# Weight preparation of a second FFN tied to program order, its output weights split at use, and token pairs in another order

## The chip, the cores and the metric

The kernel runs on one core of one Trainium2 chip. The metric is the device time of one execution in microseconds (us); lower is better.

## The reference, cut to what matters

```python
a = attention(q, mean_pool8(k), mean_pool8(v))      # 8 batches, 8 heads, 576 tokens, width 64
x = a as (4608 tokens, 512)
h = x @ w_in;  x = max(0.01 * h, h) @ w_out         # first FFN, 512 -> 2048 -> 512
xn = x / sqrt(mean(x * x) + 1e-6) * rms_g
g, val = xn @ w_gate, xn @ w_val                    # second FFN, 512 -> 1536
out = (g * sigmoid(g) * val) @ w_out2               # 1536 -> 512
```

The activations are fp32. The weights arrive as 64-bit floats, and the kernel turns them into fp32 itself.

## The kernel before, in words

Every product is made of three matmuls of rounded parts: a number is kept as a high part (an fp32r copy) and a low part (the rest), and `TERMS` names high x high, high x low and low x high. `split` (L89) makes the two parts: a copy on ACT for the high one, a subtraction on POOL or DVE for the low one.

**First stage.** Nine tiles of 512 tokens (loop at L1090). In each, 16 jobs `f`: `h_unit` (12 matmuls, then two activations on ACT and a subtraction on DVE) and, two jobs later, `y_unit` (12 matmuls). Attention for the coming tiles runs beside this: its steps are written into `attention_slot` (L1110), which is called twice in a job, so there are 32 slots to a tile. `y_store` ends a tile. Half of the first FFN's output weights (`wr`, L674) are loaded again in every tile from tile 2 on, so that eight of these weights take turns in four slots, and four slots are free.

**Preparation of the second FFN's weights**, `side_steps` (L682). From tile 2 on, each slot also runs one entry of a list of steps. A unit of work takes a raw tile of 64-bit words (512 KB): `start` loads it (SP), `convert` starts to make fp32 of it (an activation on ACT, L98, and a multiplication on DVE, L692), `end` merges the halves (DVE, L698) and, for gate and value weights, makes four sums (L709), `high` and `low` split into parts (ACT L735, POOL L739), and `store` writes them to DRAM (SP, L745: `op_dram` for gate and value, `wo_dram` for the output weights, here in the trace `op_g`, `op_v` and `wo`). There are 24 units for gate and value, each six slots behind the last, and 12 for the output weights, each four slots behind the last. Two slots hold raw tiles (`raws`) in turn and two (`outs`) hold parts.

**Second stage.** Five pairs of token blocks (L794): three of 2 x 512 tokens, then two of 2 x 384. For each pair there are 12 `Quad`s (6 of gate, 6 of value in turn); a quad makes seven products of six matmuls where eight would be usual (`p1` to `p7`), with the sums prepared above. Its weights come from DRAM in four loads to a quad, into ten slots `a` (`load_a`, L934). The products of a value quad become the inputs `u` of the output product, in which each of 12 `f` takes 12 matmuls (9 in a pair of 384) for each half of the pair. These are cut into `pieces` (`queue_out`, L1154), one or two of which run in a quad; the rest, the second half of the pair above all, runs after the quads, and four pieces are left for the next pair. The output weights `wo` of each `f` are loaded for each half (`load_o`, L953): 120 loads into four slots `o`, three `f` ahead. Norm and token sums of the next pair run between the products (`norm_steps`, `token_steps`).

**Order.** The program is traced in this order, and a scheduler then orders each engine's instructions by a simulated timeline; an instruction whose inputs are ready early by that timeline can be moved ahead. Each engine, and the queue of DMA issues on SP, then works in the order given, and one that waits holds up what is behind it. `keep_in_program_order(ins)` puts `ins` behind the instruction that was traced just before it on its engine, without a wait for its end.

**What the change touches:** `prelu` (L97), the copies `er` in attention's `step_x` (L362), `wo_dram` (L664), `side_steps`, `pairs`, `load_a`, `load_o`, `first_pair` (L962), `queue_out` and the loop over quads (L1162).

Of the kernel before, what the change touches and what calls it, by code (L numbers as in the profile page):

```python
# [22 lines left out]
def pooled_attention_then_two_ffns(  # L23
# [73 lines left out]
    def prelu(out, in_, alpha, scale=1.0):  # L97
        nc.scalar.activation(out=out, in_=in_, func=AF.Prelu, scale=scale, alpha=alpha)  # L98
# [248 lines left out]
    def step_x(b, t):  # L347
# [14 lines left out]
        for g in range(2):  # L362
            (nc.scalar.copy if b < 2 else nc.gpsimd.tensor_copy)(  # L363
# [300 lines left out]
    wo_dram = [dram.tile([P, 2, 512], F32, name=f"wo{f}") for f in range(F2)]  # L664
# [17 lines left out]
    def side_steps():  # L682
# [13 lines left out]
        def merge(raw):  # L696
            top, low = raw[:, :, 1], raw[:, :, 0]
            nc.vector.scalar_tensor_tensor(  # L698
                out=top, in0=top, scalar=3, in1=low, op0=ALU.logical_shift_left, op1=ALU.bitwise_or
            )  # L700
# [13 lines left out]
        def unit(begin, n, name, load, srcs_of, with_sums):  # L714
# [3 lines left out]
            def start():  # L718
                held["raw"] = raw_in_slot(raws[n % 2], f"raw_{name}")
                load(held["raw"])  # L720

            def end():
                merge(held["raw"])
                if with_sums:
                    sums(held["raw"].bitcast(F32).rearrange("p (k i n) w -> p k i n w", k=2, i=2))

            def high(z):
                t = weight_slot(outs[z], f"parts_{name}_{z}").rearrange("p h n -> p (h n)")
                held[z], o = [], 0
                for src, dst in srcs_of(held["raw"])[z]:  # L730
                    a, b = src.shape[1:]
                    d = t[:, o:o + 2 * a * b].rearrange("p (a h n) -> p a h n", a=a, h=2)
                    o += 2 * a * b
                    held[z].append((src, d, dst))
                    nc.scalar.activation(out=d[:, :, HI, :], in_=src, func=AF.Copy)  # L735

            def low(z):
                for src, d, dst in held[z]:
                    nc.gpsimd.tensor_tensor(  # L739
                        out=d[:, :, LO, :], in0=src, in1=d[:, :, HI, :].bitcast(F32), op=ALU.subtract  # L740
                    )

            def store(z):
                for src, d, dst in held[z]:
# [3 lines left out]
            at(begin + 3, lambda: convert(held["raw"]))  # L748
            at(begin + 4, end)
            for z, t0, t2 in ((0, 5, 8), (1, 7, 10)) if with_sums else ((1, 6, 9),):  # L750
                at(begin + t0, lambda z=z: high(z))
                at(begin + t0 + 1, lambda z=z: low(z))
                at(begin + t2, lambda z=z: store(z))

        begin = n = 0
        for p in range(NPAIR):
            for m, src in (("g", w_gate), ("v", w_val)):
                for c in range(2):
                    def load(raw, src=src, p=p, c=c):
                        nc.sync.dma_start(  # L760
                            out=raw.rearrange("p (k f) w -> p k (f w)", k=2),
# [467 lines left out]
```

## Time and profile before

| | us |
|---|---|
| median of 3 runs | 1883.0 |
| lowest, highest | 1882.14, 1887.19 |
| profiled execution | 1877.53 |
| its span, first to last instruction | 1875.8 |

PE is the matmul engine (TensorE), PEld its weight loads, DVE VectorE, ACT ScalarE, POOL GpSimd, SP the engine that issues DMAs; a q behind the name is an engine's sequencer. A line of code stands as L592, a tile by its name without numbers, and `out<-in` says what an instruction writes and reads. The granted clock is that of TensorE, 1.00 being 2.4 GHz. A wait is put down to what ended last before the waiting instruction began.

### The profile page before, as it was taken

What the parts mean: (1) busy time and instruction counts of PE and PEld (TensorE: products, weight loads), DVE (VectorE), ACT (ScalarE), POOL (GpSimd) and SP (SyncE); (2) the same over time, 40 slices, a digit from 0 to 9 for tenths busy, and PEclk for the clock granted to TensorE, in tenths of its full rate; (3) what the DMA queues carried; (4) which work ended last, traced back from release to release, by engine and by line L of the source; (5) the groups of instructions that cost most, each with busy time, mean ns of one, the idle gap of its engine ahead of it and who ended that gap; (6) DMA issues with size and microseconds to landing.
All of it is one profiled execution on the core that took longest, in us unless ns stands there. A gap on an engine that the chain in (4) does not pass through costs nothing.

```text
span 1875.8 us, 23874 instructions
## 1 busy us (share of the span) xinstructions
PE 1777.5 (95%) x8596; PEld 1500.1 (80%) x8596; DVE 858.4 (46%) x1533; ACT 671.3 (36%) x1424; POOL 575.7 (31%) x751
## 2 busy tenths in 40 slices
PE   4899989989999999999999999999999999999898
PEld 3789877767888888888887787878787888898886
DVE  8975457567344344343162456145513451443232
ACT  5754355454333333332343323232313232332221
POOL 2654246446213131000122432243213322330340
PEclk9999998989999999999999999999999999999999
DMA  8833268778533332212243556765676567777754
GB/s 263 291 103 97 76 205 275 239 244 264 192 99 85 97 92 82 68 46 79 90 130 123 181 180 204 248 197 185 197 244 201 182 216 256 236 241 254 236 201 157
DMA packets 173733, 330.82 MB, mean 176 GB/s; under 512 B 54320, under 2 KB 88112, under 8 KB 172848
## 3 DMA queue, kind: packets, MB, share of 16 engines
q1 hardware_dynamic: 173616, 329.31, 54.1%
q8 instruction: 68, 1.11, 0.2%
q14 instruction: 49, 0.40, 0.1%
HBM read 277.87 MB, written 51.38 MB: 176 GB/s over the span
## 4 chain that ended last, share of the span: by engine, by line
PE 71%; DMA 11%; DVE 9%; POOL 3%; issue 2%; ACT 2%; SPq 1%; POOLq 0%; ACTq 0%; DVEq 0%
PE h L592 15%; PE y L628 15%; PE o L1077 14%; PE yv L1002 5%; PE yg L1002 4%; PE xv L1002 3%; PE xg L1002 3%; PE wg L1002 3%; PE wv L1002 3%; DMA av<-op_v 2%; DMA raw_v<-in_moe_w_val_dram 2%; DMA ag<-op_g 1%; PE sc L325 1%; PE av L395 1%; DMA wo<-parts_p 1%
## 5 line engine op out<-in xcount | busy, mean ns | idle before, releaser
L592 PE MATMUL h<-xhl,w_i 128*128 128x512 f32 (+1 forms) x1824 | 438.1, 385 | 1.4 <-ACT w_i L92 0.7
L592 PEld LDWEIGHTS h<-xhl,w_i 128*128 128x128 f32 x1824 | 330.4, 191 | 65.6 <-DVE xhl L95 2.5
L1077 PE MATMUL o<-wo,u 128*128 128x512 f32 x1296 | 320.8, 392 | 10.7 <-DMA wo<-wo 4.6
L1077 PEld LDWEIGHTS o<-wo,u 128*128 128x128 f32 x1296 | 241.0, 188 | 64.9 <-DMA wo<-wo 6.1
L628 PE MATMUL y<-ghl,w_o 128*128 128x512 f32 (+1 forms) x1296 | 286.0, 366 | 1.4 <-DVE ghl L605 1.4
L628 PEld LDWEIGHTS y<-ghl,w_o 128*128 128x128 f32 x1296 | 220.0, 192 | 35.5 <-DVE ghl L605 1.8
L605 DVE TENSOR_TENSOR ghl<-g,ghl 128x512 fp32r<-128x512 f32 (+1 forms) x152 | 111.8, 736 | 203.9 <-ACT g L98 200.2
L628 PE MATMUL y<-ghl,wr 128*128 128x512 f32 x624 | 158.3, 395 | 0.0
L98 ACT ACTIVATE ghl<-h 128x512 fp32r<-128x512 f32 (+1 forms) x152 | 86.7, 570 | 167.9 <-PE h L592 164.6
L628 PEld LDWEIGHTS y<-ghl,wr 128*128 128x128 f32 x624 | 115.2, 188 | 22.5
L95 POOL TENSOR_TENSOR u<-e2g,u 128x512 fp32r<-128x512 f32 (+1 forms) x25 | 31.1, 1244 | 213.6 <-ACT u L92 213.6
L1002 PE MATMUL xv<-xa,av 128*128 128x512 f32 (+1 forms) x360 | 85.6, 371 | 7.5 <-DMA av<-op_v 7.5
L1018 POOL TENSOR_TENSOR e7g<-e7v,e7g 128x512 f32<-128x512 f32 (+1 forms) x25 | 29.5, 1179 | 204.3 <-DVE e7v L979 204.3
L1002 PE MATMUL xg<-xa,ag 128*128 128x512 f32 (+1 forms) x360 | 85.4, 370 | 7.0 <-DMA ag<-op_g 3.8
L363 POOL COPY er<-ex 128x96 f32<-128x96 f32 x60 | 18.7, 339 | 227.0 <-DVE ex L340 227.0
L92 ACT ACTIVATE u<-e7g 128x512 fp32r<-128x512 f32 (+1 forms) x30 | 17.7, 590 | 193.2 <-POOL e7g L1018 177.1
L98 ACT ACTIVATE g<-h 128x512 f32<-128x512 f32 (+1 forms) x152 | 86.7, 570 | 0.0
L229 POOL TENSOR_TENSOR v<-v 128x256 f32<-128x256 f32 (+2 forms) x84 | 56.8, 679 | 93.7 <-DMA v<-in_v_dram 91.5
L1002 PE MATMUL yg<-T,ag 128*128 128x512 f32 (+1 forms) x360 | 84.3, 368 | 0.0
L1002 PE MATMUL yv<-T,av 128*128 128x512 f32 (+1 forms) x360 | 84.1, 368 | 0.1
L1002 PEld LDWEIGHTS xv<-xa,av 128*128 128x128 f32 x360 | 65.7, 188 | 19.5 <-DMA av<-op_v 10.2
L1002 PEld LDWEIGHTS xg<-xa,ag 128*128 128x128 f32 x360 | 65.5, 188 | 19.0 <-ACT e2g L1011 3.5
(166 smaller groups left out, 2706.7 us busy)
## 6 DMA issues: line engine op xcount, KB each, us to landing
wo<-wo SPq DMA_DIRECT2D x120, 512.0 KB
av<-op_v SPq DMA_DIRECT2D x90, 512.0 KB
ag<-op_g SPq DMA_DIRECT2D x90, 512.0 KB
wr<-wo SPq DMA_DIRECT2D x52, 512.0 KB
y<-ye SPq DMA_DIRECT2D x36, 256.0 KB
op_g<-parts_g SPq DMA_DIRECT2D x36, 256.0 KB
op_v<-parts_v SPq DMA_DIRECT2D x36, 256.0 KB
out_dram<-oe SPq DMA_DIRECT2D x36, 256.0 KB
```

The lines of the kernel that those rows point to most:

```text
L95: lo_eng.tensor_tensor(out=lo, in0=src, in1=hi.bitcast(F32), op=ALU.subtract)
L98: nc.scalar.activation(out=out, in_=in_, func=AF.Prelu, scale=scale, alpha=alpha)
L229: nc.gpsimd.tensor_tensor(out=x[:, :n], in0=x[:, :n], in1=x[:, n:2 * n], op=ALU.add)
L325: nc.tensor.matmul(pt[:, i * n:(i + 1) * n], y[:, p, :], kblk[b % 2][:, p * n:(p + 1) * n], start=True, stop=True,)
L363: (nc.scalar.copy if b < 2 else nc.gpsimd.tensor_copy)(out=er[:, g].rearrange("p d (q k) -> p d q k", q=2), in_=e[:, 2 * g:2 * g + 2, P:]. ...
L395: nc.tensor.matmul(pt[:, :n], vb[b, p][:, sp].rearrange("p h d -> p (h d)"), a[:, p, mp, 0:n], start=i == 0, stop=False,)
L592: nc.tensor.matmul(pt, w[:, sp, c * P:(c + 1) * P], x[:, mp, c, :], start=c == 0 and i == 0, stop=c == n_k - 1 and i == 2,)
L605: nc.vector.tensor_tensor(out=t[:, LO, :], in0=g, in1=t[:, HI, :].bitcast(F32), op=ALU.subtract)
L628: nc.tensor.matmul(pt, w[:, sp, m * P:(m + 1) * P], g[:, mp, a - c0:a - c0 + n], start=ydone[j, a] == 1 and i == 0 and m % per_bank == 0, ...
L1002: nc.tensor.matmul(pt, wt[:, a, c, sp, :], xt[:, mp, :], start=start and c == 0 and i == 0, stop=c == 1 and i == 2, skip_group_check=not s ...
L1018: eng.tensor_tensor(out=s, in0=src, in1=s, op=ALU.mult)
L1077: nc.tensor.matmul(pt, u[:, sp, m * P:(m + 1) * P], w[:, mp, :], start=f == 0 and i == 0, stop=f == F2 - 1 and i == 2,)
```

## The change

It does five things.

1. The load of a raw tile and the activation of `convert` are put in program order. `convert` comes five slots behind the load, in the same slot as `end`; before, it came three behind, and `end` four. The parts follow from the sixth slot on.
2. The output weights of the second FFN are no longer split when they are prepared: a unit ends with the merge into a slot of `outs`, and 256 KB are stored in place of 512.
3. They are split when used: `load_o` loads 256 KB into the low half of a slot, and `split_o` makes both parts there (copy on ACT, subtraction on POOL), one `f` ahead of the matmuls. The 12 loads for the second half of the last pair go to the slots `a` behind all of `load_a`'s own; in the last two quads of the last pair one piece fewer runs each.
4. The pairs are of 512, 384, 512, 384 and 512.
5. The copies `er` of batches 2 to 7 run on DVE and not on POOL.

```diff
     def prelu(out, in_, alpha, scale=1.0):
-        nc.scalar.activation(out=out, in_=in_, func=AF.Prelu, scale=scale, alpha=alpha)
+        return nc.scalar.activation(out=out, in_=in_, func=AF.Prelu, scale=scale, alpha=alpha)
...
-            (nc.scalar.copy if b < 2 else nc.gpsimd.tensor_copy)(
+            (nc.scalar.copy if b < 2 else nc.vector.tensor_copy)(
...
-    wo_dram = [dram.tile([P, 2, 512], F32, name=f"wo{f}") for f in range(F2)]
+    wo_dram = [dram.tile([P, 512], F32, name=f"wo{f}") for f in range(F2)]
...
-            prelu(top.bitcast(F32), top.bitcast(F32), 2.0 ** 32, scale=2.0 ** -112)
+            tc.keep_in_program_order(
+                prelu(top.bitcast(F32), top.bitcast(F32), 2.0 ** 32, scale=2.0 ** -112)
+            )
...
+        def load_raw(n, name, out, src):
+            t = raw_in_slot(raws[n % 2], f"raw_{name}")
+            tc.keep_in_program_order(nc.sync.dma_start(out=out(t), in_=src))
+            return t
...
             at(begin, start)
-            at(begin + 3, lambda: convert(held["raw"]))
-            at(begin + 4, end)
-            for z, t0, t2 in ((0, 5, 8), (1, 7, 10)) if with_sums else ((1, 6, 9),):
+            at(begin + 5, lambda: convert(held["raw"]))
+            at(begin + 5, end)
+            for z, t0 in ((0, 6), (1, 8)):
                 at(begin + t0, lambda z=z: high(z))
                 at(begin + t0 + 1, lambda z=z: low(z))
-                at(begin + t2, lambda z=z: store(z))
+                at(begin + t0 + 3, lambda z=z: store(z))
+
+        def plain(begin, n, f):
+            held = {}
+
+            def start():
+                held["raw"] = load_raw(
+                    n, f"p{f}", lambda t: t.rearrange("p n w -> p (n w)"), rows(w_out2, f)
+                )
+
+            def end():
+                held["t"] = per.tile([P, 2, 512], F32, tag=f"w{outs[n % 2]}", bufs=1, name=f"plain{f}")[:, 0, :]
+                merge(held["raw"], held["t"].bitcast(I32))
+
+            at(begin, start)
+            at(begin + 5, lambda: convert(held["raw"]))
+            at(begin + 5, end)
+            at(begin + 6, lambda: nc.sync.dma_start(out=wo_dram[f], in_=held["t"]))
...
-    pairs = [(0, N), (2 * N, N), (4 * N, N), (6 * N, N - P), (8 * N - 2 * P, N - P)]
+    pairs = [(0, N)]
+    for n in (N - P, N, N - P, N):
+        pairs.append((pairs[-1][0] + 2 * pairs[-1][1], n))
...
+    a_todo += o_todo[-F2:]
+    del o_todo[-F2:]
...
+            a_count[0] += 1
+            if len(a_todo[i]) == 3:
+                load_o_into(a_todo[i], "a", i)
+                return
...
+    def load_o_into(key, kind, i):
+        t = slot(kind, i, f"wo{key[0]}_{key[1]}_{key[2]}")
+        nc.sync.dma_start(out=t[:, LO, :].bitcast(F32), in_=wo_dram[key[2]])
+        o_tiles[key] = t
+        o_whole.append((key, t))
...
+    def split_o(key):
+        for x in [x for x in o_whole if x[0] <= key]:
+            o_whole.remove(x)
+            t = x[1]
+            split(nc.scalar, t[:, HI, :], nc.gpsimd, t[:, LO, :], t[:, LO, :].bitcast(F32))
...
                 if ms[0] == 0:
                     load_o()
+                    if (q, z) == (last_q, 1):
+                        load_a()
+                    split_o(o_order[min(i + 1, len(o_order) - 1)])
                 out_part(q, z, f, ms)
...
-            if i + 1 < len(quads):
+            if i + 1 < (len(quads) if more else len(quads) - 2):
                 piece()
```

## Rows read from the trace of the kernel before

**Rows 1.** The page: busy share by engine, and TensorE's clock in 40 slices.

```profile
PE 1777.5 (95%) x8596; PEld 1500.1 (80%) x8596; DVE 858.4 (46%) x1533; ACT 671.3 (36%) x1424; POOL 575.7 (31%) x751
...
PEclk9999998989999999999999999999999999999999
```

**Rows 2.** Windows, tiles 1-5, 7: PE, PEld, DVE, ACT, POOL busy (count), clock, DMA share, GB/s.

```profile
173.70:288.50 114.80, 106.31 (x513) 87.95 (x512) 60.21 (x129) 49.83 (x118) 45.06 (x80) 0.97 0.49 145
288.50:411.80 123.30, 110.02 (x513) 89.86 (x513) 77.78 (x163) 61.84 (x149) 67.12 (x103) 0.94 0.79 252
411.80:512.90 101.10, 96.55 (x445) 79.93 (x445) 55.55 (x100) 42.98 (x99) 47.62 (x72) 0.99 0.72 234
512.90:615.10 102.20, 102.20 (x504) 85.62 (x503) 41.13 (x81) 35.28 (x79) 23.61 (x54) 1.00 0.32 97
615.10:719.20 104.10, 103.63 (x512) 86.68 (x510) 41.34 (x85) 36.09 (x84) 24.68 (x54) 1.00 0.31 93
...
823.60:920.40 96.80, 96.80 (x461) 81.10 (x460) 29.02 (x60) 27.40 (x56) 2.10 (x6) 1.00 0.20 68
```

**Rows 3.** Waits of PE in tiles 1 to 3: total us, times, longest us.

```profile
PE qt L303 <- issue: 10.2, 4, 4.0
PE xt L369 <- DVE ex L340: 8.7, 2, 5.3
PE av L395 <- DVE at L95: 5.3, 3, 2.6
```

**Rows 4.** Waits of PE in tiles 4 to 8 (512.9 to 1008 us), all of them.

```profile
PE av L395 <- DVE at L95: 1.2, 2, 0.7
```

**Rows 5.** Waits of DVE and of SP's queue, 213 to 493 us.

```profile
DVE raw_v L692 <- DMA raw_v<-in_moe_w_val_dram: 20.2, 8, 5.8
...
SPq L745 <- POOL parts_v L739: 45.3, 38, 3.8
```

**Rows 6.** Tile views of raw_g, parts_p: duration ns min/median/max, first and last start.

```profile
L760 SPq DMA_DIRECT2D raw_g<-in_moe_w_gate_dram x12: 367/381/386, 213.0 to 456.1; - x12
...
L735 ACT ACTIVATE parts_p<-raw_p x12: 657/670/694, 258.8 to 491.0; 128x512 fp32r<-128x512 f32 x12
L739 POOL TENSOR_TENSOR parts_p<-raw_p,parts_p x12: 1304/1316/1843, 259.5 to 491.8; 128x512 fp32r<-128x512 f32 x12
```

**Rows 7.** Waits of PE in the last two pairs, 1541.7 us to the end.

```profile
PE xv L1002 <- DMA av<-op_v: 7.0, 6, 1.8
PE o L1077 <- DMA wo<-wo: 4.6, 4, 1.3
PE xg L1002 <- DMA ag<-op_g: 3.0, 4, 2.5
```

**Rows 8.** Windows, columns as in rows 2: pairs 1 and 3, an output stretch, the tail.

```profile
1170.50:1359.80 189.30, 185.31 (x808) 150.56 (x807) 79.87 (x113) 58.31 (x97) 60.90 (x47) 1.00 0.63 209
...
1541.70:1698.70 157.00, 151.35 (x769) 136.48 (x768) 61.19 (x107) 47.80 (x94) 47.75 (x47) 1.00 0.72 241
...
1371.00:1391.00 20.00, 20.00 (x90) 16.58 (x89) 1.38 (x2) 0.63 (x1) 0.00 (x0) 1.00 0.64 217
...
1832.00:1875.80 43.80, 35.66 (x158) 28.38 (x156) 9.92 (x18) 3.80 (x7) 0.00 (x0) 0.99 0.48 159
```

**Rows 9.** DMA of the second stage (1008 us to the end): total, and the output weights' loads.

```profile
DMA packets 59274, 183.85 MB, mean 212 GB/s; under 512 B 6336, under 2 KB 9408, under 8 KB 58816
...
wo<-wo SPq DMA_DIRECT2D x120, 512.0 KB
```

**Rows 10.** The chain that ended last: start us, us, what.

```profile
1372.06 17.68 PE o L1077 x78
...
1827.57 2.08 PE o L1077 x9
...
1849.49 5.84 DMA wo<-wo
```

**Rows 11.** Tile view of `er`, columns as in rows 6.

```profile
L363 POOL COPY er<-ex x60: 258/267/727, 191.4 to 873.1; 128x96 f32<-128x96 f32 x60
```

More of the change, by code (lines that the diff above doesn't have):

```diff
@@ L694, in convert, with merge @@
             )
-        def merge(raw):
+        def merge(raw, out):
             top, low = raw[:, :, 1], raw[:, :, 0]
             nc.vector.scalar_tensor_tensor(
-                out=top, in0=top, scalar=3, in1=low, op0=ALU.logical_shift_left, op1=ALU.bitwise_or
+                out=out, in0=top, scalar=3, in1=low, op0=ALU.logical_shift_left, op1=ALU.bitwise_or
             )
@@ L729, in high @@
                 held[z], o = [], 0
-                for src, dst in srcs_of(held["raw"])[z]:
-                    a, b = src.shape[1:]
+                for x, dst in srcs_of(held["raw"])[z]:
+                    a, b = x.shape[1:]
                     d = t[:, o:o + 2 * a * b].rearrange("p (a h n) -> p a h n", a=a, h=2)
                     o += 2 * a * b
-                    held[z].append((src, d, dst))
-                    nc.scalar.activation(out=d[:, :, HI, :], in_=src, func=AF.Copy)
+                    held[z].append((x, d, dst))
+                    nc.scalar.activation(out=d[:, :, HI, :], in_=x, func=AF.Copy)
@@ L758, in side_steps @@
                 for c in range(2):
-                    def load(raw, src=src, p=p, c=c):
-                        nc.sync.dma_start(
-                            out=raw.rearrange("p (k f) w -> p k (f w)", k=2),
-                            in_=src[:, p * 2 * W:(p + 1) * 2 * W].rearrange("(k c p) f -> c p k f", k=2, p=P)[c],
-                        )
                     def srcs(raw, m=m, p=p, c=c):
@@ L771, in srcs @@
                         )
-                    unit(begin, n, f"{m}{p}_{c}", load, srcs, True)
+                    operands(
+                        begin, n, f"{m}{p}_{c}", lambda t: t.rearrange("p (k f) w -> p k (f w)", k=2),
+                        src[:, p * 2 * W:(p + 1) * 2 * W].rearrange("(k c p) f -> c p k f", k=2, p=P)[c], srcs,
+                    )
                     begin += 6
@@ L776, in side_steps @@
             for f in (2 * p, 2 * p + 1):
-                def load(raw, f=f):
-                    nc.sync.dma_start(out=raw.rearrange("p n w -> p (n w)"), in_=rows(w_out2, f))
-                def srcs(raw, f=f):
-                    x = raw.bitcast(F32)[:, :, 1].unsqueeze(1)
-                    return None, ((x, wo_dram[f].rearrange("p h n -> p (h n)").unsqueeze(1)),)
-                unit(begin, n, f"p{f}", load, srcs, False)
+                plain(begin, n, f)
                 begin += 4
@@ L927, in token_steps @@
         ]
+    last_q = len(pairs) - 1
     a_todo = [(q, p, m, s) for q in range(len(pairs)) for p in range(NPAIR) for m in "gv" for s in range(4)]
+    o_todo = [(q, z, f) for q in range(len(pairs)) for z in range(2) for f in range(F2)]
+    a_todo += o_todo[-F2:]
+    del o_todo[-F2:]
     a_tiles = {}
     a_count = [0]
+    o_tiles = {}
+    o_count = [0]
+    o_whole = []
     def load_a():
@@ L975, in first_pair @@
             when.setdefault(13 + i // 2, []).append(load_o)
+        when.setdefault(15, []).append(lambda: split_o((0, 0, 0)))
         return when, late
@@ L1152, in piece @@
             pieces.pop(0)()
+    o_order = [(q, z, f) for q in range(len(pairs)) for z in range(2) for f in range(F2)]
     def queue_out(q, z, f):
```

27 lines of the change are left out of this document (9 added, 18 removed).

## The prediction

> **What bounds the kernel now.** I read the page first. TensorE is busy for 95% of the span and its granted clock is full in all slices but a few [rows 1]. So what can be won is what TensorE loses, and other engines matter only where they make it wait. The row of clocks shows where to look: the dents lie in the first half, around slices 6 to 10.
>
> Next the windows, one to a tile of the first FFN, from the first matmul of a tile's `h` to that of the next. Tiles 1 to 3 are long; tiles 4, 5 and 7 are calm (tile 6 is like tile 5), with TensorE busy throughout at clock 1.00 [rows 2]. Tiles of a like number of TensorE instructions can be compared: tile 5 has 512 in 104.1 us. Tile 1 has 513 and takes 114.8, 10.7 more; tile 2 has 513 and takes 123.3, 19.2 more. Tile 3 has 445. Between tiles 5 and 7 an instruction is worth (104.1 - 96.8) / (512 - 461) = 0.14 us, so 445 would take 94.5, and 101.1 is 6.6 more. **Tiles 1 to 3 lose 36.5 us.**
>
> The waits of TensorE in these tiles say how. Attention's transposes and products waited 10.2 + 8.7 + 5.3 = 24.2 us [rows 3], against 1.2 us in tiles 4 to 8 [rows 4]. The rest is clock: 0.97, 0.94 and 0.99 of the three tiles are 3.4 + 7.4 + 1.0 = 11.9 us. The two make 36.1, so the loss is accounted for twice over: stalls, and the lower clock in the stretches around them.
>
> What runs there and not in the calm tiles is the preparation of the second FFN's weights. Its first load is issued at 213 us and the last `gate` load at 456 [rows 6], though program order puts the first at the start of tile 2 (288.5 us) and the last early in tile 8. The scheduler has moved it up and packed it. DMA share in tile 2 is 0.79 against 0.31 in tile 5 [rows 2]. On DVE's in-order queue the first operation on a raw tile stood waiting for its load, 20.2 us in 8 waits for `raw_v` alone, and SP stood behind stores whose POOL half was not done, 45.3 us for `parts_v` alone [rows 5]. Attention's softmax, and its loads of q, are queued behind these.
>
> In the second stage the windows by pair show two kinds. A pair of 512 columns moves 209 GB/s, one of 384 columns 241 GB/s [rows 8], since weights are loaded whole for less work. In the last two pairs, both of 384, TensorE waits on loads for 7.0 + 4.6 + 3.0 = 14.6 us [rows 7]. The last 43.8 us hold only 35.66 us of TensorE work [rows 8], and the chain that ended last goes through two loads of `wo` there, one of 5.84 us [rows 10].
>
> **Part 1: the preparation is pinned.** The loads (SP) and the `convert` activation (ACT) are ordered behind what was traced before them. The rest of each unit hangs on these by data. 36 units of 6 or 4 slots are 192 slots, 32 to a tile: six tiles and two slots of the seventh, some 630 us in place of 280. Each unit keeps its instructions, except that the 12 of `w_out` lose their split (ACT 670 ns, POOL 1.316 us [rows 6]) and half of their store. `convert` is now five slots, 16 us of a 104 us tile, behind its load, and so no longer arrives before it. What was late next was attention; the calm tiles show that attention alone fits under TensorE. What stays of the 36.5 us is bounded by 0 and by the density: 280 / 630 = 0.44 of it, 16 us. I take 5, since the DMA engines are a third busy in these tiles and there is room between arrivals. **Gain 31.5 us, between 20 and 36.5.** The pinned load also holds nothing back on SP that is due sooner: behind it in program order stand loads of later slots. If the ACT queue comes to a pinned `convert` whose load is late, the `h` activations behind it wait, and TensorE has two units of `h` (12 matmuls each, 2.7 us) before it would feel it.
>
> **Part 2: `er` copies from POOL to DVE.** 60 copies of 267 ns [rows 11]. On DVE the trace has none; between 0 (it fills a wait) and 60 x 0.27 = 16 us of DVE time in tiles where DVE is busy for 41 of 104 us [rows 2]. Taken at nothing for TensorE. It spares a hop, and POOL is free for the pinned units' work.
>
> **Part 3: `wo` halves, split when used.** 120 loads [rows 9] go from 512 to 256 KB, 31 of the second stage's 184 MB. Each now needs an ACT copy and a POOL subtraction: by the same shapes' rows 0.67 and 1.32 us [rows 6], so 80 us of ACT and 158 us of POOL over 865 us. In the second pair POOL is busy for 61 of 189 us and ACT for 58 [rows 8]; 24 splits add 32 and 16 there. They fit by amount. They have to fit by latency where only `o` products are left. There one `f` of a 512 pair is 12 matmuls, 17.68 / 78 x 12 = 2.72 us, and one of a 384 pair is 9, 2.08 us [rows 10]; POOL and ACT are all but idle in such a stretch, 0.00 and 0.63 of 20 us [rows 8]. With four slots a load may be issued three `f` ahead: 8.2 or 6.2 us for the load and 2.0 us of split. Cost: nothing where the load lands within 4.2 us, up to one split (2.0 us) at each of the four pair boundaries where POOL has other work, so 0 to 8; I take 2.
>
> Gain: at the old pace a 384 pair would move 24 x 0.262 = 6.3 MB less in 157 us, 201 GB/s; run without waits (about 140 us) 225, between the pair with hardly a wait (209) and the one with waits (241). I keep 3 of the 14.6 us. **Gain 11.6 us less 2, between -8 and 15.**
>
> A rule speaks against this. The Trainium skill, "DMA: Bandwidth & Descriptors", section "Anatomy of one DMA", gives a transfer a fixed cost of about 2.0 us and only the rest by bytes. By it, as an estimate, a `wo` load would fall only from 3.2 to 2.6 us; if latency and not rate made the waits, this part would give a fifth of the 14.6, 3 us, in place of 11.6.
>
> **Part 4: pairs 512, 384, 512, 384, 512.** The same number of columns and of matmuls, so nothing in TensorE time; two more loads of `xst`, hidden by the quads around them. It puts a light pair behind each heavy one and a light one last, which is part of the 11.6. **Part 5: the last pass's `wo` in the `a` slots, two pieces kept back.** Ten of twelve loads then come before the tail. The tail loses 43.8 - 35.66 = 8.1 us, some 3 of them the last copy and store; the 4.6 us of `wo` waits is already in the sum, nothing is added.
>
> **Sum.** 31.5 + 11.6 - 2 = 41 us. The profiled execution took 1877.5 us, 1.7 more than its span; less 41 this is 1836.5. The median of the runs, 1883.0, lies 5.5 above the profiled one, so 1842.
>
> **The rivals.** *The pin doesn't hold* (0.12): it ties an instruction only to the one just before it on its engine, and if that one (a load of q, say) is itself moved up, the preparation stays packed. For it: SP's loads have few ties. Against: the instruction before a pinned `convert` is often the `h` activation, which can't run before its matmuls. Then part 1 gives some 5 us and the rest 10: 1868.
>
> *Part 3 gives nothing* (0.08): the waits for loads are latency. For it: single `wo` loads of 5.84 us on the chain [rows 10] while the tail moved little. Against: the waits sit in the pairs with the highest rate. Then 1883 - 31.5 = 1851. The skill's fixed cost, above, would make it so.
>
> *Slower* (0.08): load and split together become the bound of the `o` stretches. The place is the 12 `f` of the second half of each pair but the last, whose loads come early. Load 5.84, split 2.0, and one POOL operation of 1.3 ahead of it make 9.1 us; this is 2.9 over the 6.2 us of a 384 pair and 0.9 over the 8.2 of a 512 pair: 24 x 2.9 + 24 x 0.9 = 91 us, so 1883 - 31.5 + 91 = 1942. It outweighs part 1 from a chain of some 7.5 us on (24 x 1.3 = 31). Against: the load is halved and the engines are idle there.
>
> **The numbers.** The forecast has 0.72. A measurement of this kernel can tell some 0.3%, 5.6 us, from no change. The forecast and the first two rivals are all faster, together 0.92; 0.04 of it goes to no change, where the pin fails and the split costs what it saves: 0.88. The low end takes both gains whole: 1883 - 36.5 - 15 = 1831, and 1829 for the small waits beside them. The high end takes 20 us for part 1 and a loss of 2 for part 3: 1865. It leaves out the failing pin and the slower case, together 0.2.
>
> **What would show it.** Loads of raw tiles from the start of tile 2 to tile 8; tiles 1 to 3 at 104, 104 and 95 us (a little more for tile 3), clock 1.00, no waits of `qt` and `xt`. In the second stage waits on `av`, `ag` and `wo` of 3 us in all, and a new wait of `o` on POOL (the split) of 2. Wrong if raw loads still begin before 270 us, if tiles 4 to 7 grow by over 2 us each, or if `o` waits on POOL for over 8 us.

## The result and the profile after

The changed kernel is slower: 1912.4 us (median of 4 runs, 1909.2 to 1916.2) against 1884.5 for the kernel before, ratio 1.0149, 95% interval 1.0124 to 1.0173. The forecast was 1842, in a range of 1829 to 1865.

The page after, head and busy shares; they answer to [rows 1]. ACT has 61 us more work and POOL 124, and TensorE's share is a point lower.

```profile
span 1914.5 us, 24149 instructions
...
PE 1795.0 (94%) x8596; PEld 1506.2 (79%) x8596; DVE 883.7 (46%) x1593; ACT 732.2 (38%) x1532; POOL 699.6 (37%) x799
```

The windows by tile of the kernel after (columns as in [rows 2]), tiles 1 to 7:

```profile
173.10:278.90 105.80, 103.84 (x514) 86.71 (x512) 44.50 (x92) 34.82 (x81) 22.05 (x41) 1.00 0.20 54
278.90:384.10 105.20, 103.40 (x513) 86.79 (x512) 55.48 (x124) 43.28 (x105) 33.47 (x60) 1.00 0.48 154
384.10:482.60 98.50, 95.80 (x446) 79.00 (x445) 41.41 (x88) 34.66 (x79) 31.75 (x52) 1.00 0.47 150
482.60:595.50 112.90, 105.30 (x504) 87.59 (x503) 58.85 (x118) 43.12 (x99) 34.38 (x60) 0.97 0.49 153
595.50:706.50 111.00, 106.28 (x512) 88.40 (x511) 57.86 (x124) 44.87 (x107) 33.44 (x60) 0.97 0.49 151
706.50:816.60 110.10, 107.52 (x513) 89.47 (x511) 56.53 (x125) 44.50 (x106) 18.25 (x32) 0.96 0.42 131
816.60:913.40 96.80, 96.80 (x460) 81.11 (x460) 41.74 (x94) 36.45 (x78) 11.19 (x16) 1.00 0.47 158
```

Tiles 1, 2 and 3 are shorter by 9.0, 18.1 and 2.6 us than in [rows 2]: the pin holds, and the preparation is no longer packed into them but runs on to tile 8. But tiles 4 and 5 are longer by 10.7 and 6.9, and tile 6 by 5.7 (104.4 us before), at a clock of 0.97 and 0.96 where it was 1.00. The second stage begins at 1001.3 us in place of 1008.3: 7 us are left of 36.

The second stage as one window, from the first matmul of its first quad to the last copy of its output, for the kernel before and after:

```profile
1008.30:1872.70 864.40, 831.77 (x3833) 701.92 (x3831) 334.88 (x518) 247.95 (x438) 260.62 (x223) 1.00 0.64 212
```

```profile
1001.30:1911.50 910.20, 851.06 (x3833) 708.62 (x3831) 345.45 (x518) 314.74 (x555) 413.51 (x339) 0.99 0.53 168
```

It is 46 us longer, with fewer bytes (168 GB/s in place of 212), with 67 us more of ACT and 153 more of POOL, against 80 and 158 that were worked out. TensorE's own busy time is 19 us longer for the same 3833 instructions, at a clock of 0.99 in place of 1.00; the rest are waits. **So the first stage gained little and the second lost much.** Two views tell where.

First, the waits of PE in tiles 4 to 6 after, and of DVE between 278 and 905 us:

```profile
PE xt L369 <- DVE ex L340: 7.6, 2, 5.8
PE xr L374 <- DVE er L363: 6.1, 3, 2.1
```

```profile
DVE raw_v L695 <- DMA raw_v<-in_moe_w_val_dram: 42.2, 10, 5.9
DVE raw_p L695 <- DMA raw_p<-in_moe_w_out_dram: 36.8, 12, 6.5
DVE raw_g L695 <- DMA raw_g<-in_moe_w_gate_dram: 36.4, 12, 5.2
```

DVE stands waiting for raw loads 34 times, 115 us in all. Only the ACT half of `convert` is pinned; its DVE multiplication was put right behind the load, where by the scheduler's timeline the load has landed. The timeline of such a place, which holds the longest wait of `xt`:

```profile
514.52 0.46 SPq L719 DMA_DIRECT2D raw_v<-in_moe_w_val_dram  x1
...
519.05 0.43 DVE L695 TENSOR_SCALAR raw_v<-raw_v 128x512 int32<-128x512 uint32 x1 [4.99 <-DMA raw_v<-in_moe_w_val_dram]
519.39 0.20 DVE L339 RECIPROCAL st<-st 128x8 f32<-128x8 f32 x1
519.62 0.76 DVE L340 TENSOR_TENSOR ex<-ex,st 128x576 f32<-128x576 f32 x1
520.41 0.41 DVE L363 COPY er<-ex 128x96 f32<-128x96 f32 x2
520.53 0.87 PE L369 MATMUL xt<-ident,ex 128*128 128x128 f32 x3 [5.75 <-DVE ex L340]
```

The softmax (L339, L340) and the copies `er`, now on DVE too, are queued behind a multiplication whose result is not used before 555.2 us, when the merge begins, 36 us later, and TensorE waits 5.75 us for them. (Just before, L338 had held DVE for 2.91 us where 0.17 is usual; see the last section.)

Second, the second stage: the waits of PE, and the longest of ACT (the kernel before has no wait of ACT for `wo`).

```profile
PE xv L1035 <- DMA av<-op_v: 11.7, 8, 3.1
PE xg L1035 <- ACT e1g L1063: 7.5, 7, 1.3
PE xg L1035 <- ACT e2g L1044: 7.1, 2, 3.7
PE yv L1035 <- DVE e7v L1012: 5.6, 5, 1.8
PE xg L1035 <- ACT rms L873: 5.3, 2, 2.7
```

```profile
ACT wo L92 <- DMA wo<-wo: 181.2, 68, 8.4
```

`av` is waited for no less than before (7.5 us) though the rate has fallen, and new waits stand behind ACT: in all, TensorE waits 57.6 us in this stage in place of 31.1, behind ACT 26.8 in place of 4.3 and behind loads 15.3 in place of 15.9. The timeline of one, in the first pair of 384:

```profile
1224.00 0.63 ACT L92 ACTIVATE wo<-wo 128x512 fp32r<-128x512 f32 x1 [3.96 <-DMA wo<-wo]
1224.64 1.28 ACT L873 ACT_TABLE_LOAD   x1
...
1225.94 0.69 ACT L873 ACTIVATE rms<-ms,eps 128x512 f32<-128x512 f32 x1
...
1226.68 2.29 PE L1035 MATMUL xg<-xa,ag 128*128 128x384 f32 x6 [2.58 <-ACT rms L873]
```

The copy of the split stands 3.96 us in ACT's queue until its load lands; `rms`, which has to empty the bank that the next `xg` writes, is behind it, and a table load of 1.28 us, which the kernel before has too, comes between them.

### The profile page after: what moved, and what is told of

Its sections match the earlier page's. It is cut to its first block, busy times and chain, and to the rows that moved or that the text cites. A ratio compares the mean times of both kernels' runs of the same rounds, so it can differ in the third digit from the quotient of the medians.

```text
span 1914.5 us, 24149 instructions
## 1 busy us (share of the span) xinstructions
PE 1795.0 (94%) x8596; PEld 1506.2 (79%) x8596; DVE 883.7 (46%) x1593; ACT 732.2 (38%) x1532; POOL 699.6 (37%) x799
## 4 chain that ended last, share of the span: by engine, by line
PE 67%; DMA 14%; DVE 9%; POOL 5%; ACT 2%; issue 2%; SPq 1%; POOLq 0%; ACTq 0%; DVEq 0%
PE h L592 16%; PE y L628 15%; PE o L1110 12%; PE yv L1035 4%; PE yg L1035 4%; PE xv L1035 3%; PE xg L1035 3%; PE wg L1035 3%; PE wv L1035 3%; DMA wo<-wo 2%; DMA av<-op_v 2%; DMA v<-in_v_dram 2%; PE sc L325 1%; DMA ag<-op_g 1%; DMA raw_v<-in_moe_w_val_dram 1%
## 5 line engine op out<-in xcount | busy, mean ns | idle before, releaser
L1110 PE MATMUL o<-wo,u 128*128 128x512 f32 x1296 | 325.7, 395 | 12.9 <-POOL u L95 2.9
L95 POOL TENSOR_TENSOR wo<-wo 128x512 fp32r<-128x512 f32 x120 | 159.8, 1334 | 316.2 <-ACT wo L92 315.6
L92 ACT ACTIVATE wo<-wo 128x512 fp32r<-128x512 f32 x120 | 75.4, 630 | 264.0 <-DMA wo<-wo 186.0
L1035 PE MATMUL xg<-xa,ag 128*128 128x512 f32 (+1 forms) x360 | 91.0, 387 | 23.6 <-ACT e1g L1063 7.5
L229 POOL TENSOR_TENSOR v<-v 128x256 f32<-128x256 f32 (+3 forms) x84 | 56.0, 673 | 123.6 <-DMA v<-in_v_dram 121.8
L1035 PEld LDWEIGHTS yv<-T,av 128*128 128x128 f32 x360 | 66.9, 190 | 10.3 <-DVE e1g L1012 0.9
L245 POOL TENSOR_TENSOR kp<-k 128x64 f32<-128x64 f32 x70 | 27.1, 412 | 129.2 <-PE kt L283 129.1
```

Of the source, the lines that this page charges most:

```text
L92: nc.scalar.activation(out=hi, in_=src, func=AF.Copy)
L95: lo_eng.tensor_tensor(out=lo, in0=src, in1=hi.bitcast(F32), op=ALU.subtract)
L229: nc.gpsimd.tensor_tensor(out=x[:, :n], in0=x[:, :n], in1=x[:, n:2 * n], op=ALU.add)
L245: nc.gpsimd.tensor_tensor(out=t[:, j, :], in0=x[:, 0:D], in1=x[:, D:2 * D], op=ALU.add)
L1035: nc.tensor.matmul(pt, wt[:, a, c, sp, :], xt[:, mp, :], start=start and c == 0 and i == 0, stop=c == 1 and i == 2, skip_group_check=not s ...
L1110: nc.tensor.matmul(pt, u[:, sp, m * P:(m + 1) * P], w[:, mp, :], start=f == 0 and i == 0, stop=f == F2 - 1 and i == 2,)
```

## The experiments

All medians can be compared: the kernel before, run beside each group, gave 1882.5 to 1884.5. The second stage is the window defined above, of one profile each, and begins where the first ends.

| kernel | median us | ratio to before (95%) | stage 2 begins | stage 2 |
|---|---|---|---|---|
| before (second profile) | 1883 | 1 | 1008.3 (1010.3) | 864.4 (871.9) |
| after | 1912.4 | 1.0149 (1.0124 to 1.0173) | 1001.3 | 910.2 |
| e1 part 1 alone | 1869.7 | 0.9928 (0.9904 to 0.9951) | 988.7 | 879.9 |
| e2 after, no split at use | 1875.9 | 0.9960 (0.9940 to 0.9981) | 994.5 | 876.4 |
| e3 after, old pairs | 1885.1 | 1.0011 (0.9991 to 1.0032) | 1000.7 | 881.5 |
| e4 after, split's copy pinned | 1900.8 | 1.0084 (1.0052 to 1.0115) | 999.9 | 896.2 |
| e5 after, DVE half pinned | 1895.9 | 1.0074 (1.0045 to 1.0103) | 989.4 | 904.3 |
| e6 after, er on POOL | 1901.2 | 1.0102 (1.0071 to 1.0132) | 992.3 | 903.3 |
| e7 before, both pins | 1867.0 | 0.9923 (0.9898 to 0.9948) | 983.9 | 878.1 |
| e10 no split, old pairs | 1871.7 | 0.9942 (0.9923 to 0.9961) | 990.4 | 878.3 |
| e11 half load, no split | 1883.1 | 1.0000 (0.9987 to 1.0013) | 1002.5 | 878.6 |
| e12 e2 + idle split | 1894.5 | 1.0063 (1.0039 to 1.0086) | 991.2 | 900.4 |
| e13 e2 + idle copy | 1890.8 | 1.0040 (1.0021 to 1.0059) | 988.8 | 889.1 |
| e14 half load, old pairs | 1878.5 | 0.9970 (0.9952 to 0.9989) | 1002.9 | 871.8 |
| e15 e10 + idle split | 1893.6 | 1.0041 (1.0022 to 1.0060) | 992.7 | 897.6 |
| e16 all pins, old pairs | 1868.8 | 0.9915 (0.9886 to 0.9945) | 985.7 | 878.3 |
| e17 all pins, new pairs | 1886.4 | 1.0011 (0.9994 to 1.0029) | 985.3 | 898.9 |

### Parts undone or alone

e1, on the kernel before: the two pins and the later steps of part 1; the units of `w_out` keep their split, in slot `outs[n % 2]`.

```diff
-            prelu(top.bitcast(F32), top.bitcast(F32), 2.0 ** 32, scale=2.0 ** -112)
+            tc.keep_in_program_order(
+                prelu(top.bitcast(F32), top.bitcast(F32), 2.0 ** 32, scale=2.0 ** -112)
+            )
...
-            at(begin + 3, lambda: convert(held["raw"]))
-            at(begin + 4, end)
-            for z, t0, t2 in ((0, 5, 8), (1, 7, 10)) if with_sums else ((1, 6, 9),):
+            at(begin + 5, lambda: convert(held["raw"]))
+            at(begin + 5, end)
+            for z, t0, t2 in ((0, 6, 9), (1, 8, 11)) if with_sums else ((1, 6, 9),):
```

> Part 1 alone: the kernel before with the load and the convert activation pinned and the steps five slots behind, the output weights still split when prepared, pairs and second stage as before. The changed kernel began its second stage 7 us earlier than the kernel before (tiles 1 and 2 shorter by 27, tiles 4 to 6 longer by 23), so if part 1 acts as it did there, the ratio is 0.996 (7 us faster, within 4) and the second stage takes as long as before. The rival, that the later stage suffers from where the preparation lands, expects 10 us or more above the kernel before.

Measured 13 us faster, and the second stage begins 20 us earlier: more than the 7 expected. So something else in the change costs the first stage some 12 us. The windows of tiles 1 to 6 in e1:

```profile
174.00:280.40 106.40, 104.35 (x513) 87.38 (x512) 42.22 (x83) 34.89 (x81) 24.36 (x52) 0.99 0.20 55
280.40:386.60 106.20, 104.32 (x512) 87.48 (x512) 51.63 (x112) 43.52 (x106) 35.13 (x70) 0.99 0.47 152
386.60:484.10 97.50, 95.52 (x446) 78.99 (x445) 41.22 (x84) 36.14 (x82) 36.69 (x59) 1.00 0.48 160
484.10:589.70 105.60, 103.16 (x505) 85.30 (x505) 56.59 (x108) 44.02 (x102) 40.23 (x72) 1.00 0.52 165
589.70:697.10 107.40, 104.46 (x513) 86.79 (x512) 54.52 (x115) 45.00 (x109) 38.19 (x71) 0.99 0.51 161
697.10:803.70 106.60, 106.14 (x512) 88.53 (x512) 53.39 (x115) 45.30 (x109) 24.85 (x44) 0.98 0.44 140
```

Tiles 1 to 3 gain 29.1 us, and tiles 4 to 6 lose 8.9. The second stage, whose instructions come in the same order as in the kernel before, took 879.9 us.

e2, on the kernel after: output weights split when prepared, whole loads.

```diff
-            at(begin + 6, lambda: nc.sync.dma_start(out=wo_dram[f], in_=held["t"]))
+            at(begin + 6, high)
+            at(begin + 7, low)
+            at(begin + 9, lambda: nc.sync.dma_start(out=wo_dram[f], in_=held["t"].bitcast(F32)))
...
-        nc.sync.dma_start(out=t[:, LO, :].bitcast(F32), in_=wo_dram[key[2]])
+        nc.sync.dma_start(out=t.bitcast(F32), in_=wo_dram[key[2]])
...
-        o_whole.append((key, t))
```

> The changed kernel with part 3 undone: output weights split when prepared and loaded whole, all else changed. Theory A (the loss of 46 us in the second stage comes from the split at use, whose ACT copy stands in ACT's in-order queue waiting 181 us in all for its load): 40 us or more below the changed kernel, some 1868. Theory B (the order of the pairs makes it): stays within 10 us of the changed kernel, above 1902.

36 us faster than the kernel after, 34 of it in the second stage. Theory A's direction, a little under its size.

e3, on the kernel after:

```diff
-    pairs = [(0, N)]
-    for n in (N - P, N, N - P, N):
-        pairs.append((pairs[-1][0] + 2 * pairs[-1][1], n))
+    pairs = [(0, N), (2 * N, N), (4 * N, N), (6 * N, N - P), (8 * N - 2 * P, N - P)]
```

> The changed kernel with the pairs of the kernel before (three of 512, then two of 384), the split at use kept. Theory A (the split's copy waits on ACT): within 10 us of the changed kernel, 1905 to 1922, with the 384 pairs again the slow ones. Theory B (the order of the pairs): 40 us less, some 1872.

27 us faster, between the marks of the two theories (1905 and 1872): theory B has much right too. Split and order cost 36 and 27 us, each in the presence of the other, more than the whole loss together.

e4, on the kernel after:

```diff
-            split(nc.scalar, t[:, HI, :], nc.gpsimd, t[:, LO, :], t[:, LO, :].bitcast(F32))
+            tc.keep_in_program_order(
+                nc.scalar.activation(out=t[:, HI, :], in_=t[:, LO, :].bitcast(F32), func=AF.Copy)
+            )
+            nc.gpsimd.tensor_tensor(
+                out=t[:, LO, :], in0=t[:, LO, :].bitcast(F32), in1=t[:, HI, :].bitcast(F32), op=ALU.subtract
+            )
```

> The changed kernel with the ACT copy of the split at use pinned in program order too, so that it does not stand in ACT's queue ahead of its load; the same work. Theory A (the wait in ACT's queue costs): ACT's waits for wo fall from 181 us to under 60, and the time by 25 us or more, to some 1885. Rival C (the work itself, 80 us of ACT and 160 us of POOL, or the latency of load and split, costs): within 10 us of the changed kernel or slower.

ACT's wait for `wo` in e4's second stage:

```profile
ACT wo L993 <- DMA wo<-wo: 72.0, 33, 6.7
```

Of 181 us of waiting 109 are gone, and 12 us of time (14 of the second stage); neither expectation is met. TensorE's waits behind ACT fall from 26.8 to 10.2 us, those behind loads and DVE rise by 5 and 7. The wait in ACT's queue is a cause, and what this pin takes away of it is a third of the split's price.

### The first stage

e5, on the kernel after:

```diff
-            nc.vector.tensor_scalar(
+            tc.keep_in_program_order(nc.vector.tensor_scalar(
                 out=low, in0=low.bitcast(U32), scalar1=0.9374 * 2.0 ** -29, scalar2=None, op0=ALU.mult
-            )
+            ))
```

> The changed kernel with convert's other half, the DVE multiplication of the raw tile, pinned in program order as well. In the changed kernel it stood right behind its load and DVE waited for it 36 times, 115 us in all, with attention's softmax behind it. Theory D (this wait is what tiles 4 to 6 still lose): the waits fall under 20 us, tiles 4 to 6 take 104 us each in place of 111, and the time falls by 15 to 20 us, to some 1894. Rival E (the tiles lose by something else, such as the er copies on DVE or POOL holding DVE): the same time within 6 us though the waits are gone.

The waits of DVE for raw loads in e5 (all of them), and its tiles 4 to 6:

```profile
DVE raw_g L695 <- DMA raw_g<-in_moe_w_gate_dram: 3.6, 1, 3.6
...
DVE raw_v L695 <- DMA raw_v<-in_moe_w_val_dram: 2.8, 1, 2.8
```

```profile
487.20:591.30 104.10, 102.63 (x504) 85.49 (x503) 62.27 (x119) 43.75 (x101) 34.64 (x60) 1.00 0.53 166
591.30:698.60 107.30, 103.87 (x513) 86.57 (x511) 60.83 (x124) 44.10 (x107) 33.87 (x60) 1.00 0.50 156
698.60:804.20 105.60, 105.14 (x511) 87.86 (x511) 55.61 (x124) 44.21 (x106) 19.84 (x32) 0.98 0.42 136
```

Theory D holds: 115 us of waiting (34 waits, not 36) become 6, tiles 4 to 6 fall from 334.0 to 317.0 us, the second stage begins 12 us earlier, and the time falls by 16.5. In the kernel before these tiles take 310.7.

e6, on the kernel after:

```diff
-            (nc.scalar.copy if b < 2 else nc.vector.tensor_copy)(
+            (nc.scalar.copy if b < 2 else nc.gpsimd.tensor_copy)(
```

> The changed kernel with the er copies of batches 2 to 7 back on POOL. Rival E for the er copies (they load DVE where it is late): 6 us or more below the changed kernel, tiles 4 to 6 at 106. If they cost nothing: within 5 us of it, or slower.

11 us faster, 9 of them before the second stage begins: the copies on DVE cost something. They stand there behind the waits for raw loads (`xr <- DVE er` above; e5 has no such wait and keeps them on DVE), so the two causes may overlap: both edits together (e17) take 16 us off the first stage, alone 12 and 9. But first stages of the same order of instructions differ by 4 us (e2 and e10), and the overlap is no larger than that by much.

e7 is e1 with e5's pin.

> The kernel before with part 1 and the DVE multiplication pinned too; output weights split when prepared, pairs as before. Theory D: second stage begins some 30 us earlier than in the kernel before (part 1 alone gave 20), and the ratio is 0.985, some 1855. Rival E: as part 1 alone, 0.993.

The second stage begins 24 us earlier than before (expected 30), 5 earlier than in e1. The time is 1867.0, ratio 0.9923: rival E's mark of 0.993 lies in the interval and theory D's 0.985 does not, and the intervals of e1 and e7 overlap. So here the second pin gives little if anything, although DVE waits 106 us for raw loads in e1, nearly as long as in the kernel after. The sum of the waits is not their price; what stands behind them decides.

### The second stage

e10 is e2 with the edit of e3.

> The changed kernel with part 3 undone and the old pairs: the fourth corner beside the changed kernel (1912), the one without the split (1876) and the one with old pairs (1885). If split and order add up, it is 27 under the one without the split: 1849. If each harms by using up the same slack, the two losses overlap less without the other and it lies at 1865 to 1875, no more than 11 below.

1871.7, as the second of the two has it: without the split the new order costs 4 us, no more than the noise (the intervals of e2 and e10 overlap), and not 27. Split and order don't add up. The second stage takes 878.3 us with neither (e10), 881.5 with the split alone (e3), 876.4 with the new order alone (e2), and 910.2 with both; the first three as windows, in this order:

```profile
990.40:1868.70 878.30, 838.86 (x3833) 707.34 (x3831) 335.04 (x518) 248.32 (x438) 260.85 (x223) 0.99 0.63 209
```

```profile
1000.70:1882.20 881.50, 841.43 (x3833) 702.60 (x3831) 343.91 (x518) 313.40 (x554) 412.34 (x339) 1.00 0.54 173
```

```profile
994.50:1870.90 876.40, 834.95 (x3833) 702.84 (x3831) 334.94 (x518) 247.85 (x439) 261.54 (x223) 1.00 0.63 209
```

Yet ACT waits even longer for `wo` in e3 than the 181 us of the kernel after:

```profile
ACT wo L92 <- DMA wo<-wo: 229.6, 80, 8.4
```

So a wait in ACT's queue is not dear in itself. With the new order the split's price is spread over all five pairs: each is 5 to 9 us longer in the kernel after than in e2.

e11, on the kernel after (the split has nothing in its place):

```diff
-            split(nc.scalar, t[:, HI, :], nc.gpsimd, t[:, LO, :], t[:, LO, :].bitcast(F32))
...
-                    pt, u[:, sp, m * P:(m + 1) * P], w[:, mp, :],
+                    pt, u[:, sp, m * P:(m + 1) * P], w[:, LO, :],
```

> The changed kernel with the 256 KB loads of the output weights kept and the split at use left out; all three matmuls of a term read the loaded half, so the product with the low part of these weights is not computed as it should be, at the same number and size of matmuls. It has what the halved load gains and none of what the split costs. The prediction's rate view (half the bytes take away the waits for av, ag and wo): 12 us under the kernel without the split (1876), some 1864. The view that these waits are latency: 1872 to 1876.

The time of the whole, 1883.1, meets neither expectation, since the first stage ends 8 us later than e2's. The second stage takes 878.6 us against 876.4 with whole loads. The first pair of 384 columns as a window, in e2 and in e11:

```profile
1155.40:1322.00 166.60, 153.66 (x767) 136.39 (x767) 66.32 (x109) 50.37 (x94) 51.38 (x47) 1.00 0.70 231
```

```profile
1166.40:1333.40 167.00, 155.28 (x768) 137.90 (x767) 68.16 (x111) 50.40 (x94) 51.58 (x47) 0.99 0.60 194
```

The rate falls from 231 to 194 GB/s and the pair takes as long. With these pairs the rate was not what made TensorE wait. (The first stage ends at 1000 to 1003 us in all kernels here whose output weights are prepared without a split, with `er` on DVE and the DVE half not pinned, and at 989 to 995 where they are split in preparation; DVE's waits for raw loads are 102 to 120 us in both. Why is open.)

e12 and e13, on e2, whole loads; e13 has the first two of these lines alone:

```diff
+            junk = p2.tile([P, 512], mybir.dt.bfloat16, tag="junk", bufs=1, name=f"junk{key[0]}_{key[1]}_{key[2]}")
+            nc.scalar.activation(out=junk, in_=t[:, LO, :].bitcast(F32), func=AF.Copy)
+            nc.gpsimd.tensor_tensor(out=junk, in0=t[:, LO, :].bitcast(F32), in1=junk, op=ALU.subtract)
```

> The kernel without the split at use (whole loads, 1876), with a copy on ACT and a subtraction on POOL of each loaded tile added, at the place and of the size of the split, into a tile of 16-bit floats that nothing reads; no matmul waits for it. Theory A (the queues are held: ACT stands waiting for the load, POOL is busier): most of the 36 us appears though no matmul waits for a split, 1900 or more. Rival F (the chain of load, copy and subtraction ahead of the matmul is what is late): within 10 us of 1876.

> The same with the copy on ACT alone, without the subtraction on POOL. Theory A with ACT's wait as its cause: as much as with both, within 8 us. If POOL's work is what costs: within 8 us of the kernel without the split (1876).

The longest wait of ACT (in sum) in e12's second stage:

```profile
ACT junk L1004 <- DMA wo<-wo: 253.9, 80, 8.9
```

The second stage grows by 24.0 us with copy and subtraction and by 12.7 with the copy alone, though no matmul waits for either; by the medians of the whole it is 18.6 and 14.9 us. e12's 1894.5 lies between the marks of theory A (1900) and rival F (1886): half of the 36 us or more comes without a matmul that waits for the split. e13 is 3.6 us from e12, within the 8 that speak for ACT's wait as the cause. How much POOL's work adds is not settled: e13's profile is of the fastest of its six executions, 1882.7. Nor can what is left of the 34 us be put down to the matmuls' dependence, since e12's loads are whole and ACT waits 254 us there in place of 181.

The kernel before, once more:

> The kernel before once more, for a second profile. The kernels with old pairs and the unchanged second stage took 878 to 880 us for it in their profiles against 864 in the first profile of the kernel before, at the same order of instructions there. If the first profile was a lucky one: 870 or more here. If the shorter first stage itself costs the second one: 864 again, within 3.

871.9 us, so by this mark the first profile was a lucky one. Its row:

```profile
1010.30:1882.20 871.90, 837.09 (x3833) 705.97 (x3831) 334.85 (x518) 247.86 (x438) 260.50 (x223) 0.99 0.64 210
```

The order of instructions is the same as in the first profile. Of the 7.5 us TensorE's busy time has 5.3, at a clock of 0.99 in place of 1.00, and waits for `av` were 9.5 us in place of 7.5. e1 and e7 have this order in the second stage too and took 879.9 and 878.1. So one order of instructions took 864 to 880 us; that a shorter first stage costs the second one something is not excluded. A stage difference of less than some 15 us between two profiles proves nothing by itself here, and medians of the whole decide.

e14 is e11 with old pairs, e15 is e12 with old pairs.

> The changed kernel with old pairs, the 256 KB loads kept and the split at use left out, all three matmuls reading the loaded half (the product with the low part of these weights is not computed as it should be). With the new pairs the halved load gained nothing (second stage 878 us against 876 with whole loads). If it gains where a 384 pair comes last, as the last pair of the kernel with split and old pairs suggests (170 us against 180): second stage 867 or less, and the time 10 us or more under the changed kernel with old pairs (1885), some 1872. If it gains nothing here either: second stage 878, the time 1880 or more.

> The kernel without the split at use and with old pairs (1872, second stage 878), with the idle copy on ACT and subtraction on POOL added as with the new pairs, where they cost 24 us of the second stage. If the cost lies in the 384 pairs that prepare a pair of 512: under 8 us here, second stage up to 886. If it lies in every pair alike: some 24 again, second stage 900.

e14's second stage is 6.5 us shorter than e10's, within that spread; the last pair of 384 takes 172.5 us against 180.4. A gain from the halved load is possible there, and not proved; the time, 1878.5, lies between the two expectations. e15's grows by 19.3 us, its median by 22: the idle split's price is much the same with either order, so it does not lie in the 384 pairs that prepare a pair of 512. The real split's price is not the same: with the old pairs 3.2 us against e10 and 9.7 against e14, with the new ones 33.8 against e2 and 31.6 against e11. So the idle split with its whole loads is no measure of the real one.

e16 and e17 have e4's and e5's pins and e6's edit, with old and new pairs.

> The changed kernel with old pairs, er back on POOL, and both the DVE multiplication of convert and the ACT copy of the split pinned: each cause found taken away. First stage as in the kernel before with both pins (second stage begins at 984 us); second stage 881 us without the pin of the copy. If that pin gives 10 to 15 us here as with the new pairs: some 1855, below all kernels so far. If it gives nothing with old pairs: some 1867.

> The same with the new pairs. Second stage 895 us, as with the pin of the copy alone, after a first stage that ends at 984: some 1881, 30 us under the changed kernel, if the first stage's and the second's losses are apart. If the order of the pairs is no handicap once nothing stands waiting in the queues: within 8 us of the same with old pairs.

e16 takes 1868.8 us, 14.9 less than the kernel before and 43.6 less than the changed one, but no less than e7, which keeps whole loads and the split in preparation: with old pairs the pin of the copy gives nothing. e17 takes 1886.4, far more than 8 us above e16, and near the first of its two expectations. The first stages are alike (985.7 and 985.3), and the second stages still differ by 20.6 us:

```profile
985.70:1864.00 878.30, 839.61 (x3833) 702.79 (x3831) 346.04 (x518) 309.91 (x557) 417.98 (x342) 1.00 0.55 174
```

```profile
985.30:1884.20 898.90, 845.97 (x3833) 710.73 (x3831) 350.34 (x518) 310.45 (x557) 417.07 (x342) 0.98 0.54 171
```

Of these, 14.3 us are waits of TensorE (51.2 in place of 36.9, those for `av` alone 16.4 in place of 9.1) and 6.4 its longer busy time, at a clock of 0.98 in place of 1.00. ACT still waits 62.9 us for `wo` in e17, and 46.7 in e16. So the handicap of the new order in the presence of the split is not the wait of an unpinned copy alone. Its cause stays open.

## Why the prediction was wrong, point by point

**The step that failed.** The sum took the split at use as a term of 2 us and the order of the pairs as one of 0, each by itself. By itself each costs about that: second stages of 881.5 and 876.4 us against 878.3 with neither. Together they cost 32 us (910.2), and nothing in the prediction asked what one does beside the other. The gain of 11.6 us from the halved loads did not come either, and the first stage gained 7 us in place of 31.5.

**What bounded the kernel: right.** Tiles 1 to 3 lost some 36 us to the packed preparation; with it spread out they take 105.8, 105.2 and 98.5 us at clock 1.00, where 104, 104 and 95 were expected.

**Part 1: mis-sized, 31.5 us where part 1 alone gave 20 and the change 7.** In e1 tiles 1 to 3 gain 29.1 us, nearly what was forecast, but the tiles behind them, where the preparation now runs, lose 9: 16 us of the 36.5 stay, the bound that the prediction had worked out from the density, where it took 5. A reason given was that `convert`, five slots behind its load, "no longer arrives before it". This holds for its ACT half. The DVE half has no tie but its data, and the scheduler put it right behind the load: 115 us of DVE waits, more than the 51 us of the kernel before (20.2 + 17.0 + 13.7, the first of them in [rows 5]). With both halves pinned part 1 gives 24 us (e7), so this half explains at most some 5 us of what is missing in e1, and 12 in the first stage of the changed kernel (e5). What the change loses beyond e1 goes with `er` on DVE (below) and with the preparation without a split, which ends the first stage 7 us later than the one with it (after and e2; 10 in e3 and e10). The prediction had this as less work, and why it costs is open. The mark set beforehand, tiles 4 to 7 longer by over 2 us each, was met by tiles 4 to 6.

**Part 2, `er` on DVE: taken at nothing, worth 9 to 11 us in the changed kernel (e6).** Its cover was DVE's idle time, and DVE's queue stood waiting for loads.

**Part 3: the gain did not come, and the cost was mis-sized by a factor of 16 beside the new order.** Bytes and work were right: 153.8 MB are moved in the second stage in place of 183.9, and ACT and POOL have 67 and 153 us more. The gain of 11.6 us rested on the view that TensorE's waits for loads go with the rate; e11 takes 37 GB/s away and gains nothing. The Trainium skill's fixed cost of a transfer ("DMA: Bandwidth & Descriptors", "Anatomy of one DMA"), cited against this part, goes in the direction that e11 shows: its estimate was 3 us in place of 11.6, and the measured second stage is 2.2 us longer, within the spread. That section of the page is on transfers that GpSimd issues, while `wo` is issued by SP, and no run here shows the fixed cost itself. The cost of 2 us looked only at whether the split is ready when a matmul needs it. Measured are 32 us with the new pairs (910.2 against 878.6 for the same loads without the split; 29 by the medians), and 10 with the old ones (e3 and e14), within the spread of one profile. Where it is dear, TensorE waits behind ACT: 26.8 us in place of 4.3 in the kernel before, and 10.2 once the copy is pinned (e4). What a waiting `convert` on ACT would hold up was asked in part 1; what a waiting split would hold up was not asked in part 3, and there it is the copies, activations and `rms` that free the banks of PSUM. With the old pairs TensorE waits behind ACT too (18.0 us in e3, 5.1 in e10), but there its waits behind loads fall from 22.9 to 6.9 us, and the sum stays at 38. With the new pairs they fall only from 17.6 (e2) to 15.3. So in one profile each the halved loads paid for the split in the old order and not in the new one.

**Part 4, the order: taken at nothing or a small gain.** Without the split it costs 4 us (e2 and e10), which is not clear of the noise, with it 27 (e3). That it matters only beside the split was not foreseen, and is not explained.

**Part 5, `wo` of the last pass in the `a` slots: taken at nothing, and worth nothing that shows.** e10 has it, with whole loads and the old pairs, and its second stage of 878.3 us is that of e1 and e7 (879.9 and 878.1), which don't.

**The clock.** The sum started from a profile whose second stage ran at clock 1.00 throughout, and took the clock of that stage as given. In the kernel after it is 0.99, and 19 of the 46 us are longer busy time of TensorE, some 9 of them by that clock; no term had such a loss. In the second profile of the kernel before the clock is 0.99 too, so not all of it belongs to the change.

**The rivals.** "Slower" had the right sign and 0.08, by a mechanism that the runs don't bear out: the `o` matmuls wait for the split's copy for 2.1 us in all, where 91 were worked out. So its sign was luck. "The pin doesn't hold" is refuted: raw loads begin at 277 us and go on to 888. "Part 3 gives nothing" was right as far as it went.

## What to carry to other kernels

Where a scheduler orders instructions by a simulated timeline, look for each instruction that waits for nothing but a load: it will be put where the load lands in the simulation, and what the load is late by is paid by all that is queued behind it on that engine. Pin both halves of such a step, or move it to where its load is surely there. The sum of such waits is not their price: 230 us of ACT's waiting went with a loss of 3 to 10 us in one order of the pairs, and 181 us with one of 32 in another. So cost work that starts with a load by what stands behind it in the queue, test two changes of one stage together as well as apart, and take a lower transfer rate for a gain only where the waits follow the rate.

## What was not expected of the hardware

A tiny operation of DVE can last as long as POOL's work beside it. The view of L338 in the kernel after, and the timeline of its longest case:

```profile
L338 DVE TENSOR_SCALAR st<-st x40: 158/172/2906, 22.6 to 864.8; 128x8 f32<-128x8 f32 x40
```

```profile
511.15 2.91 DVE L338 TENSOR_SCALAR st<-st 128x8 f32<-128x8 f32 x1
...
511.44 2.59 POOL L745 TENSOR_TENSOR parts_g<-raw_g,parts_g 128x256 fp32r<-128x256 f32 x4
```

Eight elements a partition, 0.17 us in the median, took 2.91 us and ended when POOL's four subtractions did (511.15 + 2.91 = 514.06; 511.44 + 2.59 = 514.03). It had begun while POOL was in an earlier subtraction (L229, to 511.49 us). All nine cases of over 0.4 us in this trace begin while POOL works and end 0.02 to 0.03 us behind an operation of POOL. The Trainium skill, "SBUF — State Buffer", section "SBUF: two separate sides", says that a DVE instruction in a mode that uses two ports, or with two inputs in SBUF, shares a pair of ports with GpSimd, that whichever starts first has the pair for its whole instruction, and that the other is fully blocked. These rows agree with the blocking, and here DVE was held through five instructions in a row; that the ports are the reason is not tested by any run here.
